# Two attentions on one core: how the second one's K is loaded, its scores are grouped and its Q is laid out

## The chip, the cores and the metric

The kernel runs on one core of a Trainium2 chip. The metric is the device time of one execution in microseconds (us); lower is better. The time before is 901.6 us, the median of three runs (900.64, 901.60 and 902.88).

## What is computed

Two attention blocks, A and B, work on separate inputs; their outputs stand side by side in the result. Both have 16 batches of 32 query tokens, model width 1024, 32 query heads of width 128, and a cache of 1024 keys. All tensors are bf16. A has 4 key/value heads, each shared by 8 query heads; B has 32.

```python
# B; A is the same, with k and v of each of 4 heads repeated for 8 query heads
q = (x @ wq).reshape(B, Sq, H, Dh).transpose(0, 2, 1, 3)
scores = einsum("bhqd,bhkd->bhqk", q, k_cache) * (Dh ** -0.5)
p = softmax(scores, axis=-1)
o = einsum("bhqk,bhkd->bhqd", p, v_cache)
b = o.transpose(0, 2, 1, 3).reshape(B, Sq, H * Dh) @ wo
return concatenate([a, b], axis=-1)
```

B's K and V are 134 MB each, A's 17 MB each; with the weights, the core's DMA engines read 337.64 MB from HBM (page).

## The kernel before

**The unit of work.** Scores of one "quad" fill 128 partitions (4 heads or head-batch pairs, of 32 query tokens each) by 1024 keys. Each attention has 128 quads. In A a quad is 4 query heads of one batch that share a key/value head; in B it is 2 batches times 2 heads, each with its own K and V. The steps of a quad are: scores on TensorE into one of two score buffers in PSUM (`ps_s`, two banks each, used in turn by all quads in the order in which they are recorded, `SBuf`), maximum on VectorE (`st_max`, L837), exponential with row sum on ScalarE (`st_exp`, L850), transposition of P on TensorE (L862), copy to SBUF (`st_pev`, through the helper at L526), P times V on TensorE (L884 for A, L892 for B), reciprocal (L901), scaling (L908 or L909), transposition of O (L914), copy (L526). After every 4 B quads or 8 A quads, `oproj` (L680) multiplies by a slice of `wo` and adds into an SBUF accumulator (L691, L694).

**B's scores before.** The head width has to be on partitions. `st_dmaK` loads, for one batch and two heads, 512 KB as 128 rows of 4096 B (16 keys per partition), two such loads to a quad. `KB_sb` holds 4 of them. VectorE transposes 32x32 blocks of 4-byte words (`st_ktrB`, L785; two instructions to a quad) into `KBt_sb`, which is double buffered by quad. After that the 128 elements of a head lie in two groups of 32 partitions and in two 2-byte halves, so that scores are sums of four matmuls on 32x32 tiles of the array: 32 matmuls of 512 columns to a quad (L827), recorded as 4 operations of 8. Their stationary rows, `QR`, need Q in the same broken-up order. `qprojB` (L616) computes Q with tokens on partitions (`Qtok`), `qprepB_tr` transposes it in 32x32 blocks on VectorE (`QBt`, L625; 32 times in all), and `qprepB_sh` moves it to the row groups by matmuls with the identity (L638, 512 matmuls of 256 columns), copied out to `QR` by ScalarE or VectorE (L526).

**V, A and weights.** V of a B quad comes in two loads of 512 KB with rows of 2048 B (L763), three quads deep. A's K and V are 256 KB loads with rows of 2048 B, two deep. `wq` comes in pieces with rows of 1024 B (L579), `wo` in rows of 2048 B.

**What sets the order.** The kernel records all operations with the buffers that they read and write. `list_schedule` then plays them through with a table of durations (`DUR`), of DMA costs by row size (`PACKET`), priorities (`PRIO_BONUS`) and a price for changing between matmul tile shapes (`PE_MODE`, `MODE_SWITCH`). The result is a fixed order on each engine; "any" operations get ScalarE or VectorE. Each engine executes its list in order and waits on semaphores where a buffer isn't ready. All loads are issued by SyncE (SP) in one list: a load whose buffer is not free holds up the loads behind it. A load is recorded when the last user of its buffer is: K behind the transposition, V behind the quad that has it last.

The main loop takes, per step, one B quad (`quadB_all`), about one A quad (`stepA`; A ends after 97% of the steps), a piece of Q preparation and projections, and weight loads.

Of the kernel before, what the change touches and what calls it, by code (L numbers as in the profile page):

```python
# [17 lines left out]
NKB_SLOTS = 2  # L18
# [7 lines left out]
PRIO_BONUS = {}  # L26
PE_MODE = {"scoresB": 2, "Qshuf": 2, "PVB": 1}
MODE_SWITCH = 0.05
# [8 lines left out]
    "OT_tr": (0.056, 0.22), "KTA_tr": (0.45, 0.22), "Qshuf": (0.107, 0.20), "qprojA": (0.432, 0.20), "qprojB": (0.432, 0.20),  # L37
    "oprojA": (0.432, 0.20), "oprojB": (0.432, 0.20), "xT_tr": (0.45, 0.22),
    "exp": (1.10, 0.12), "PT_ev@act": (0.466, 0.13), "norm@act": (0.25, 0.13), "OT_ev@act": (0.11, 0.13), "KTA_ev@act": (0.466, 0.13),
    "qA_ev@act": (0.47, 0.13), "qB_ev@act": (0.478, 0.13), "QR_ev@act": (0.252, 0.13), "acc0@act": (0.47, 0.13), "acc0@dve": (0.58, 0.12), "xT_ev@act": (0.90, 0.13),  # L40
    "o_fin@act": (0.47, 0.13),
    "KBt_tr": (1.126, 0.11), "max": (1.12, 0.11), "recip": (0.06, 0.11), "norm@dve": (0.23, 0.13), "PT_ev@dve": (0.58, 0.12),
    "OT_ev@dve": (0.08, 0.12), "KTA_ev@dve": (0.58, 0.12), "QBt_tr": (0.345, 0.10), "acc+": (0.58, 0.12), "accF": (0.59, 0.12),
    "qA_ev@dve": (0.58, 0.12), "qB_ev@dve": (0.58, 0.12), "xT_ev@dve": (0.60, 0.12), "o_fin@dve": (0.58, 0.12), "QR_ev@dve": (0.30, 0.12),
# [3 lines left out]
PACKET = {"kb_dma": (4096, 0.159), "wq_dma": (1024, 0.046)}  # L48
PACKET_DEFAULT = (2048, 0.084)
# [381 lines left out]
def build(nc, pa, pb, out):  # L431
# [34 lines left out]
    with stack:  # L466
# [7 lines left out]
        zeros = sb("zeros", [P, P], BF)  # L474
        id32 = sb("id32", [P, P], F32)
        z32 = sb("z32", [P, P], F32)
# [4 lines left out]
        Qtok = sb("Qtok", [P, 2, NG, CW], BF)  # L481
        QBt = sb("QBt", [P, CW], BF)
        QR = sb("QR", [P, 2, 4, 2, Dh], BF)
# [5 lines left out]
        KB_sb = sb("KB_sb", [P, 2 * NKB, 16 * Dh], BF)  # L489
        KBt_sb = sb("KBt_sb", [P, 2, 2, 16 * Dh], BF)  # L490
# [17 lines left out]
        if HOOK is not None:  # L508
            print("sbuf bytes remaining per partition:", nc.sbuf_bytes_remaining() if callable(nc.sbuf_bytes_remaining) else nc.sbuf_bytes_remaining)

        pr.add("pool", lambda g: g.memset(zeros[:], 0.0), writes=["zeros"], name="c0")
        pr.add("pool", lambda g: g.affine_select(ident[:], zeros[:], [[1, P]], ALU.not_equal, 1.0, base=0, channel_multiplier=-1),
               reads=["zeros"], writes=["ident"], name="c1")
        pr.add("pool", lambda g: g.memset(z32[:], 0.0), writes=["z32"], name="c0")
        pr.add("pool", lambda g: g.affine_select(id32[:], z32[:], [[1, P]], ALU.not_equal, 1.0, base=0, channel_multiplier=-1),
               reads=["z32"], writes=["id32"], name="c1")
# [90 lines left out]
        def qprojB(m_, G):  # L607
            lazy_flush(("wq", 1, m_))

            JS = 2 if DJ % 2 == 0 else 1  # L610
            v = Virt("bank", "pj")
            for j0 in range(0, DJ, JS):
                def e_qp(e, j0=j0):
                    last = None
                    for j in range(j0, j0 + JS):
                        last = e.matmul(bank(v)[:, 0:CW], xT_sb[:, 1, j, G * P:(G + 1) * P], wq_sb[:, 1, j, :], start=(j == 0), stop=(j == DJ - 1))  # L616
                    return last
                pcs = sorted(set(j * WQP // DJ for j in range(j0, j0 + JS)))
                pr.add("pe", e_qp, reads=[("wq", 1, k_) for k_ in pcs] + [("xT", 1, G)], writes=[v], claims=[("Qtok", m_ % 2, G)], name="qprojB", dur=0.225 * JS,
                       rtag=dict((("wq", 1, k_), m_) for k_ in pcs))  # L620
            evac(Qtok[:, m_ % 2, G, :], lambda: bank(v)[:, 0:CW], reads=[], writes=[v, ("Qtok", m_ % 2, G)], name="qB_ev",
                 wtag={("Qtok", m_ % 2, G): m_}, mul=scale)

        def qprepB_tr(m_, G):
            pr.add("dve", lambda e: e.transpose(QBt[:, :].bitcast(F32), Qtok[:, m_ % 2, G, :].bitcast(F32)),  # L625
                   reads=[("Qtok", m_ % 2, G)], writes=["QBt"], name="QBt_tr", rtag={("Qtok", m_ % 2, G): m_}, wtag={"QBt": (m_, G)})

        def qprepB_sh(m_, G, a_list):
            gp = (m_ * NG + G) % 2
            for a in a_list:  # L630
                v = Virt("bank", "pj")

                def e_sh(e, a=a, v=v):
                    last = None
                    for rg in range(4):
                        e_ = rg // 2
                        rhs = QBt[32 * a:32 * a + 32, :].rearrange("p (hp e x) -> p e hp x", hp=2, e=2)[:, e_, :, :]
                        last = e.matmul(bank(v)[32 * rg:32 * rg + 32, 0:2 * Dh].rearrange("p (hp x) -> p hp x", hp=2),  # L638
                                        ident[32 * a:32 * a + 32, 32 * a:32 * a + 32], rhs, start=True, stop=True,
                                        tile_position=(32 * a, 32 * rg))  # L640
                    return last
                pr.add("pe", e_sh, reads=["QBt", "ident"], writes=[v], claims=[("QR", gp, a)], name="Qshuf", rtag={"QBt": (m_, G)})
                evac(QR[:, gp, a, :, :], lambda v=v: bank(v)[:, 0:2 * Dh].rearrange("p (hp x) -> p hp x", hp=2), reads=[],
                     writes=[v, ("QR", gp, a)], name="QR_ev", wtag={("QR", gp, a): (m_, G)})

# [74 lines left out]
        def mk_quadB(t):  # L720
# [10 lines left out]
            q.kvslot = t % 2  # L731
            q.krslot = t % NKB
            q.vslot = t % NVB
            q.first_of_group = (jb == 0)
# [5 lines left out]
        def st_dmaK(q, t_=None):  # L740
# [6 lines left out]
            else:  # L747
                sl = (2 * q.t + t_) % (2 * NKB)
                ksrc = pb["k"][q.b0 + t_, q.h0:q.h0 + 2].rearrange("hh (p s) d -> (hh p) (s d)", s=16)
                pr.add("sp", lambda e: e.dma_start(KB_sb[:, sl, :], ksrc), writes=[("KB", sl)], dma_key=f"kb{sl}", name="kb_dma", dur=2 * Sk * Dh * 2, wtag={("KB", sl): q.kid})  # L750
# [31 lines left out]
        def st_ktrB(q, t_):  # L782
            sl = q.kvslot
            rs = (2 * q.t + t_) % (2 * NKB)
            pr.add("dve", lambda e: e.transpose(KBt_sb[:, sl, t_, :].bitcast(F32), KB_sb[:, rs, :].bitcast(F32)),  # L785
                   reads=[("KB", rs)], writes=[("KBt", sl, t_)], name="KBt_tr", rtag={("KB", rs): q.kid}, wtag={("KBt", sl, t_): q.kid})
# [8 lines left out]
        def st_scores(q):  # L795
# [3 lines left out]
            q.vbt, q.vbo = Virt("bank"), Virt("bank")  # L799
            vS = q.vS  # L800
            if q.pi == 0:
                sl = q.kvslot
                qt = QT_sb[:, q.s % 2]

                for u in range(2):
                    pr.add("pe", lambda e, u=u: e.matmul(ps_s[:, vS.idx, u, :], qt[:, q.b, q.hh0:q.hh0 + 4, :].rearrange("p a q -> p (a q)"),  # L806
                                                         KTA_sb[:, sl, u * 512:(u + 1) * 512], start=True, stop=True),
                           reads=[("QT", q.s % 2, q.hh0 + a) for a in range(4)] + [("KTA", sl)], writes=vS.res, name="scoresA", dur=0.225,
                           tag="A%d" % q.t, rtag=dict([(("QT", q.s % 2, q.hh0 + a), q.s) for a in range(4)] + [(("KTA", sl), q.kid)]))
            else:  # L810
                sl = q.kvslot
                gp = (q.m * NG + q.G) % 2

                def e_s(e, fp):
                    last = None
                    if True:
                        f, pd = fp // 2, fp % 2
                        o0 = f * 64 + pd
                        for t_ in range(2):
                            a = 2 * q.bp + t_  # L820
                            for hh in range(2):
                                cg = 2 * t_ + hh
                                for g2 in range(2):
                                    rg = 2 * hh + g2
                                    lhsT = QR[32 * rg:32 * rg + 32, gp, a, q.hp, o0:o0 + 63:2]
                                    rhs = KBt_sb[32 * rg:32 * rg + 32, sl, t_, :].rearrange("p (s x) -> p s x", s=16)[:, :, o0:o0 + 63:2]
                                    last = e.matmul(ps_s[32 * cg:32 * cg + 32, vS.idx, g2, :].rearrange("p (s j) -> p s j", s=16), lhsT, rhs,  # L827
                                                    start=(fp == 0), stop=(fp == 3), tile_position=(32 * rg, 32 * cg))
                    return last
                for fp_ in range(4):  # L830
# [105 lines left out]
        def nextA(t, k):  # L936
            later = [u for u in newA if u > t]
            return quadsA[later[k - 1]] if len(later) >= k else None

        def quadB_all(q):  # L940
            t = q.t
            for t_ in range(2):
                st_ktrB(q, t_)
                if t + NKB < NIT:
                    st_dmaK(quadsB[t + NKB], t_)
# [41 lines left out]
        for t_ in range(2):  # L987
            st_dmaK(quadsB[0], t_)
# [136 lines left out]
```

## Time and profile before

| quantity | value |
|---|---|
| median of three runs | 901.6 us |
| profiled execution: its span, first to last instruction | 902.6 us |
| instructions | 29455 |
| ScalarE / VectorE / TensorE busy | 610.8 / 745.3 / 836.3 us |
| loads and stores | 341.67 MB, mean 379 GB/s |
| K loads of B, issue to landing (median) | 9.2 us |
| V loads of B, issue to landing (median) | 8.1 us |
| mean granted TensorE clock | 0.985 |

The page of the profile gives the profiled execution by its span only; nothing that lies around it is recorded, so that the span stands for its time. It is 1.0 us over the median of the runs.

How to read it: a busy share is an average over the span. TensorE's matmuls are pipelined, so its busy time includes the depth of the pipeline. "DMA share" in a table of windows is the mean busy share of 16 DMA engines; it can pass 1 since packets overlap a little. A packet is one row of a load. The chain of waits goes back from the last instruction, step by step, to what released it.

### The profile page before, as it was taken

The numbers are of one execution on the slowest core, as the hardware profiler recorded it, in microseconds if no ns is written. First come the engines' busy times: TensorE is split into PE (matmuls) and PEld (weight loads), VectorE is DVE, ScalarE is ACT, GpSimd is POOL, SyncE is SP. The second block draws the span as 40 slices with busy tenths as digits, with TensorE's granted clock in tenths as the row PEclk, the third lists the DMA queues.
The fourth block names the chain that finished last, engine by engine and source line by source line (L and its number), as shares of the span: only waits on it lengthen the run. The fifth ranks groups of instructions, "written<-read, shape, count | busy, mean of one in ns | idle before, by whom it ended". The sixth has DMA issues, their size and how long they took to land.

```text
span 902.6 us, 29455 instructions
## 1 busy us (share of the span) xinstructions
PE 836.3 (93%) x12864; PEld 481.8 (53%) x12864; DVE 745.3 (83%) x1057; ACT 610.8 (68%) x1384; POOL 1.1 (0%) x8
## 2 busy tenths in 40 slices
PE   6999999999899999999999998999998988999886
PEld 4365555555555555555545455555555554555453
DVE  0578897888887999689887899878979788798885
ACT  3477886677666776676776466776867666586763
POOL 0000000000000000000000000000000000000000
PEclk9999999999999999999999999999999999999999
DMA  9999999999999999999999999999999999999994
GB/s 325 383 389 393 386 385 392 390 393 383 392 387 389 393 380 388 380 386 376 387 385 391 394 369 389 388 393 370 388 387 391 392 391 367 344 393 393 393 377 170
DMA packets 153984, 341.67 MB, mean 379 GB/s; under 512 B 12544, under 2 KB 28928, under 8 KB 153856
## 3 DMA queue, kind: packets, MB, share of 16 engines
q1 hardware_dynamic: 153856, 339.79, 100.6%
q8 instruction: 102, 1.67, 0.8%
q14 instruction: 26, 0.21, 0.1%
HBM read 337.64 MB, written 2.10 MB: 376 GB/s over the span
## 4 chain that ended last, share of the span: by engine, by line
PE 48%; DMA 23%; DVE 19%; ACT 8%; SPq 1%; issue 1%; ACTq 0%; DVEq 0%
DMA KB_sb<-in_B_k_cache_dram 21%; PE ps_s L827 10%; PE ps_g L862 9%; DVE stat L837 8%; DVE KBt_sb L785 8%; PE ps_g L680 6%; ACT P_sb L850 5%; PE ps_g L892 4%; PE ps_g L598 4%; PE ps_g L884 4%; PE ps_g L616 3%; PE ps_s L806 3%; PE ps_g L776 2%; ACT PT_sb L526 1%; PE ps_g L914 1%
## 5 line engine op out<-in xcount | busy, mean ns | idle before, releaser
L785 DVE STREAM_TRANSPOSE KBt_sb<-KB_sb 128x1024 f32<-128x1024 f32 x256 | 311.8, 1231 | 42.5 <-DMA KB_sb<-in_B_k_cache_dram 40.4
L837 DVE TENSOR_REDUCE stat<-ps_s 128x1 f32<-128x1024 f32 x256 | 304.7, 1209 | 50.7 <-PE ps_s L827 34.3
L850 ACT ACTIVATE P_sb<-ps_s,stat 128x1024 bf16<-128x1024 f32 x256 | 285.8, 1119 | 51.5 <-DVE stat L837 50.0
L862 PE MATMUL ps_g<-id,P_sb 128*128 128x128 f32 x1024 | 177.0, 300 | 13.0 <-ACT P_sb L850 4.7
L862 PEld LDWEIGHTS ps_g<-id,P_sb 128*128 128x128 f32 x1024 | 150.5, 207 | 54.9 <-issue 11.1
L827 PE MATMUL ps_s<-KBt_sb,QR 32*32 32x512 bf16 x4096 | 157.2, 399 | 19.5 <-ACT P_sb L850 10.9
L526 ACT COPY PT_sb<-ps_g 128x512 f32<-128x512 f32 x234 | 134.9, 591 | 59.5 <-PE ps_g L862 58.3
L908 ACT ACTIVATE O_sb<-ps_g,stat 128x128 bf16<-128x128 f32 x199 | 71.4, 370 | 63.0 <-PE ps_g L892 32.4
L806 PE MATMUL ps_s<-KTA_sb,QT_sb 128*128 128x512 bf16 x256 | 91.5, 388 | 6.0 <-ACT P_sb L850 5.6
L827 PEld LDWEIGHTS ps_s<-KBt_sb,QR 32*32 32x32 bf16 x4096 | 49.3, 90 | 81.1 <-ACT P_sb L850 17.8
L892 PE MATMUL ps_g<-VB_sb,PT_sb 128*32 128x128 bf16 x4096 | 91.1, 224 | 1.4 <-ACT PT_sb L526 0.9
L892 PEld LDWEIGHTS ps_g<-VB_sb,PT_sb 128*32 128x32 bf16 x4096 | 60.2, 97 | 48.7 <-issue 29.2
L884 PE MATMUL ps_g<-VA_sb,PT_sb 128*128 128x128 bf16 x1024 | 78.8, 220 | 1.8 <-ACT PT_sb L526 0.7
L884 PEld LDWEIGHTS ps_g<-VA_sb,PT_sb 128*128 128x128 bf16 x1024 | 61.6, 98 | 28.2 <-issue 8.5
L616 PE MATMUL ps_g<-wq_sb,xT_sb 128*128 128x512 bf16 x256 | 71.4, 386 | 2.9 <-DMA wq_sb<-in_B_wq_dram 2.8
L680 PE MATMUL ps_g<-woB_sb,OTB_sb 128*128 128x512 bf16 x256 | 68.7, 381 | 4.4 <-ACT OTB_sb L526 1.8
L598 PE MATMUL ps_g<-xT_sb,wq_sb 128*128 128x512 bf16 x256 | 72.0, 385 | 0.3
L680 PE MATMUL ps_g<-woA_sb,OTA_sb 128*128 128x512 bf16 x256 | 63.0, 380 | 1.3 <-DVE OTA_sb L526 1.0
L914 PE MATMUL ps_g<-ident,O_sb 128*128 128x128 bf16 x256 | 51.8, 224 | 3.0 <-ACT O_sb L908 2.0
L850 ACT ACTIVATION_READ_ACCUMULATOR P_sb<-ps_s,stat 128x1 f32 x256 | 51.8, 202 | 0.0
L526 ACT COPY OTA_sb<-ps_g 128x64 f32<-128x64 f32 x114 | 24.7, 216 | 36.7 <-PE ps_g L914 36.1
L691 DVE TENSOR_TENSOR acc<-acc,ps_g 128x512 f32<-128x512 f32 x64 | 41.2, 675 | 8.1 <-PE ps_g L680 7.6
(41 smaller groups left out, 537.5 us busy)
## 6 DMA issues: line engine op xcount, KB each, us to landing
VB_sb<-in_B_v_cache_dram SPq DMA_DIRECT2D x256, 512.0 KB, 8.1
KB_sb<-in_B_k_cache_dram SPq DMA_DIRECT2D x256, 512.0 KB, 9.2
KA_sb<-in_A_k_cache_dram SPq DMA_DIRECT2D x64, 256.0 KB, 7.7
VA_sb<-in_A_v_cache_dram SPq DMA_DIRECT2D x64, 256.0 KB, 8.1
wq_sb<-in_B_wq_dram SPq DMA_DIRECT2D x32, 256.0 KB, 8.6
wq_sb<-in_A_wq_dram SPq DMA_DIRECT2D x32, 256.0 KB, 8.8
woB_sb<-in_B_wo_dram SPq DMA_DIRECT2D x32, 256.0 KB, 9.2
woA_sb<-in_A_wo_dram SPq DMA_DIRECT2D x32, 256.0 KB, 9.1
```

The source lines that it names most:

```text
L526: return e.copy(dst, src) if hasattr(e, "activation") else e.tensor_copy(dst, src)
L598: last = e.matmul(bank(v)[:, 0:tn], wq_sb[:, 0, j, hc * Dh:(hc + 1) * Dh], xT_sb[:, 0, j, t0:t0 + tn], start=(j == 0), stop=(j == DJ - 1))
L616: last = e.matmul(bank(v)[:, 0:CW], xT_sb[:, 1, j, G * P:(G + 1) * P], wq_sb[:, 1, j, :], start=(j == 0), stop=(j == DJ - 1))
L680: last = e.matmul(bank(v)[:, 0:OUTW], OT[:, gp, hh, :], wo_[:, hh, oh * OUTW:(oh + 1) * OUTW], start=(hh == 0), stop=(hh == nh - 1))
L785: pr.add("dve", lambda e: e.transpose(KBt_sb[:, sl, t_, :].bitcast(F32), KB_sb[:, rs, :].bitcast(F32)), reads=[("KB", rs)], writes=[("KBt" ...
L806: pr.add("pe", lambda e, u=u: e.matmul(ps_s[:, vS.idx, u, :], qt[:, q.b, q.hh0:q.hh0 + 4, :].rearrange("p a q -> p (a q)"), KTA_sb[:, sl, ...
L827: last = e.matmul(ps_s[32 * cg:32 * cg + 32, vS.idx, g2, :].rearrange("p (s j) -> p s j", s=16), lhsT, rhs, start=(fp == 0), stop=(fp == 3 ...
L837: pr.add("dve", lambda e: e.tensor_reduce(stat[:, vst.idx, 0:1], ps_s[:, vS.idx, :, :], AXIS.XY, ALU.max, negate=True), writes=vS.res + [v ...
L850: return e.activation(dst, src, ACTF.Exp, bias=stat[:, vst.idx, 0:1], scale=1.0, accum_out=stat[:, vst.idx, 1:2])
L862: last = e.transpose(bank(vb)[:, m * P:(m + 1) * P], p32[:, m:Sk // 2:NPK], id32[:])
L884: last = e.matmul(bank(vb)[:, 0:Dh], ptc_of(vPT, c, 0, P), VA_sb[:, kvs, c, :], start=(c == 0), stop=(c == NCH - 1))
L892: last = e.matmul(bank(vb)[32 * a:32 * a + 32, 0:Dh], ptc_of(vPT, c, 32 * a, 32 * a + 32), VB_sb[:, kvs, a // 2, a % 2, c, :], start=(c == ...
```

## The change

K of B is loaded for one batch and four heads at once: 1 MB as 128 rows of 8192 B (32 keys per partition); `KB_sb` holds 3 of these. A pair of quads (the same two batches, heads 0-1 and 2-3 of the four) shares two loads. Their transposition is 4 instructions of the same size as before, each on one half (`u`) of the 32 keys; the read side now takes every second 4-byte word, so that after it a partition group belongs to one head. `KBt_sb` holds one pair, where it held two quads. The scores of both quads of a pair are recorded together, as 8 operations of 8 matmuls; they take both score buffers. `qprojB` makes Q with head elements on partitions straight away: `wq` is now the stationary side, taken at every fourth column, and the result is what the scores read (`QB_sb`). `Qtok`, `QBt`, `QR` and the steps that make them are gone. The order of P's columns for B changes with the keys' order (`st_exp`). Tables of the planner are changed.

```diff
-NKB_SLOTS = 2
+NKB_SLOTS = 3
-PRIO_BONUS = {}
-PE_MODE = {"scoresB": 2, "Qshuf": 2, "PVB": 1}
-MODE_SWITCH = 0.05
+PRIO_BONUS = {"max": 8, "exp": 8, "scoresA": 6, "scoresB": 6}
+PE_MODE = {"scoresB": 2, "PVB": 1}
+MODE_SWITCH = 0.1
...
-PACKET = {"kb_dma": (4096, 0.159), "wq_dma": (1024, 0.046)}
-PACKET_DEFAULT = (2048, 0.084)
+PACKET = {"kb_dma": (8192, 0.318), "wq_dma": (1024, 0.0487)}
+PACKET_DEFAULT = (2048, 0.0885)
...
-        KB_sb = sb("KB_sb", [P, 2 * NKB, 16 * Dh], BF)
-        KBt_sb = sb("KBt_sb", [P, 2, 2, 16 * Dh], BF)
+        KB_sb = sb("KB_sb", [P, NKB, 32 * Dh], BF)
+        KBt_sb = sb("KBt_sb", [P, 2, 32 * Dh], BF)
...
-        def qprojB(m_, G):
+        def qprojB(m_, fp):
...
-                        last = e.matmul(bank(v)[:, 0:CW], xT_sb[:, 1, j, G * P:(G + 1) * P], wq_sb[:, 1, j, :], start=(j == 0), stop=(j == DJ - 1))
+                        w = wq_sb[:, 1, j, fp:CW:4]
+                        last = e.matmul(bank(v)[:, 0:NTOK], w, xT_sb[:, 1, j, :], start=(j == 0), stop=(j == DJ - 1))
...
-            evac(Qtok[:, m_ % 2, G, :], lambda: bank(v)[:, 0:CW], reads=[], writes=[v, ("Qtok", m_ % 2, G)], name="qB_ev",
+            evac(QB_sb[:, m_ % 2, fp, :], lambda: bank(v)[:, 0:NTOK], reads=[], writes=[v, ("QB", m_ % 2, fp)], name="qB_ev",
...
-                sl = (2 * q.t + t_) % (2 * NKB)
-                ksrc = pb["k"][q.b0 + t_, q.h0:q.h0 + 2].rearrange("hh (p s) d -> (hh p) (s d)", s=16)
+                k = q.t + t_
+                sl = k % NKB
+                ksrc = pb["k"][q.b0 + t_, q.m * MS:(q.m + 1) * MS].rearrange("h (p s) d -> (h p) (s d)", s=32)
...
-            pr.add("dve", lambda e: e.transpose(KBt_sb[:, sl, t_, :].bitcast(F32), KB_sb[:, rs, :].bitcast(F32)),
+            c0, c1 = u * 16 * Dh, (u + 1) * 16 * Dh
+            pr.add("dve", lambda e: e.transpose(KBt_sb[:, t_, c0:c1].bitcast(F32).rearrange("p (s g i) -> p s g i", s=16, g=2),
+                                               KB_sb[:, sl, c0:c1].bitcast(F32).rearrange("p (s i g) -> p s g i", s=16, g=2)),
...
+        def st_scoresB(qs):
+            for q in qs:
+                st_slots(q)
+            def e_s(e, u, fp):
+                last = None
+                o0 = (fp // 2) * 64 + fp % 2
+                for t_ in range(2):
+                    for hh in range(2):
+                        cg = 2 * t_ + hh
+                        for q in qs:
+                            rg = 2 * q.hp + hh
+                            tok = (q.b0 + t_) * Sq
+                            lhsT = QB_sb[32 * rg:32 * rg + 32, q.m % 2, fp, tok:tok + Sq]
+                            rhs = KBt_sb[32 * rg:32 * rg + 32, t_, :].rearrange("p (s x) -> p s x", s=32)[:, 16 * u:16 * u + 16, o0:o0 + 63:2]
+                            last = e.matmul(ps_s[32 * cg:32 * cg + 32, q.vS.idx, u, :].rearrange("p (s j) -> p s j", s=16), lhsT, rhs,
+                                            start=(fp == 0), stop=(fp == 3), tile_position=(32 * rg, 32 * cg))
...
-                    dst = P_sb[:, vP.idx, :].rearrange("p (g j s) -> p g j s", g=2, s=16)
+                    dst = P_sb[:, vP.idx, :].rearrange("p (j u s) -> p u j s", u=2, s=16)
...
+        def pairB_front(n):
+            q0, q1 = quadsB[2 * n], quadsB[2 * n + 1]
+            for t_ in range(2):
+                for u in range(2):
+                    st_ktrB(q0, t_, u)
+                kdma(2 * n + t_ + NKB)
+            st_scoresB([q0, q1])
+            for q in (q0, q1):
+                st_max(q)
+                st_exp(q)
...
-            quadB_all(qB)
+            if t % 2 == 0:
+                pairB_front(t // 2)
+            quadB_back(qB)
```

## The prediction

> **What bounds the kernel now.** I read the page first: the busy rows, then the slices.
>
> ```profile
> PE 836.3 (93%) x12864; PEld 481.8 (53%) x12864; DVE 745.3 (83%) x1057; ACT 610.8 (68%) x1384; POOL 1.1 (0%) x8
> DMA  9999999999999999999999999999999999999994
> DMA packets 153984, 341.67 MB, mean 379 GB/s; under 512 B 12544, under 2 KB 28928, under 8 KB 153856
> q1 hardware_dynamic: 153856, 339.79, 100.6%
> ```
>
> Two resources look full, TensorE and the DMA engines. TensorE's figure counts pipeline depth; the DMA figure is plain: the packets of the load queue alone fill 16 engines for the whole span. The windows separate the ends from the middle:
>
> ```profile
> 0.00:15.00 15.00, 7.54 (x59) 4.41 (x60) 0.71 (x2) 6.02 (x7) 1.15 (x8) 0.99 0.88 293
> 30.00:870.00 840.00, 790.14 (x12323) 456.25 (x12323) 720.37 (x1025) 585.78 (x1336) 0.00 (x0) 0.99 1.03 386
> 622.00:626.00 4.00, 3.90 (x60) 1.84 (x59) 3.94 (x4) 1.34 (x4) 0.00 (x0) 1.00 0.72 251
> 885.00:902.60 17.60, 9.90 (x200) 5.73 (x188) 8.45 (x13) 6.45 (x16) 0.00 (x0) 0.89 0.29 103
> ```
>
> The last two columns are DMA share and GB/s. From 30 to 870 us the engines are full (1.03); single holes such as 622-626 us are rare; the end is a tail of compute. In the trace's packet records I counted, at each moment, by how much fewer than 16 packets were in flight: 2.5 us of idle before 15 us, 8.8 us from there to 885 us, 11.1 us after. That leaves 902.6 - 22.4 = 880.2 us in which the time is simply bytes over rate. The waits agree: VectorE stands 40.4 us before its K transposition for data, so compute is ahead of the loads.
>
> ```profile
> DVE KBt_sb L785 <- DMA KB_sb<-in_B_k_cache_dram: 40.4, 39, 8.6
> SPq L763 <- PE ps_g L892: 136.7, 69, 7.4
> SPq L750 <- DVE KBt_sb L785: 115.2, 77, 5.2
> ```
>
> The SP rows are loads held back until a buffer is free. With a median 9.2 us from issue to landing they mostly cost nothing; the 622-626 us hole is one that did: V waited 4.6 us at the head of SP's list and the engines ran dry.
>
> **The row size (on the path).** Stretches with almost only one kind of load give its rate:
>
> ```profile
> 33.00:35.50 2.50, 2.05 (x18) 0.86 (x15) 2.50 (x5) 1.80 (x4) 0.00 (x0) 1.00 1.09 349
> 20.20:22.70 2.50, 2.50 (x13) 1.17 (x12) 0.00 (x0) 0.00 (x0) 0.00 (x0) 1.00 1.05 386
> 24.90:27.40 2.50, 2.50 (x13) 1.08 (x12) 0.58 (x1) 0.12 (x1) 0.00 (x0) 1.00 1.03 410
> ```
>
> These are rows of 1024 B (wq), 2048 B (V) and 4096 B (K). A fit of packet counts to full stretches of 2 us over the whole trace gives 47, 85.4 and 162.8 ns a packet on one engine: 38.6 ns per KB and about 8 ns for the packet itself. On that line 8192 B cost 318 ns against 2 x 162.8 = 325.6: 7.7 ns less for each of 16,384 new packets, over 16 engines **-7.9 us**. The bounds are the only 8192 B packets in this trace, those of instruction loads on another queue: 307 ns before the stream starts (-19 us) and a median of 328 ns beside it (+2 us, no gain). I take the line, since it is the same queue and buffer; the 328 shares its engine with a second queue.
>
> The Trainium skill ("DMA: Bandwidth & Descriptors", section "Bandwidth", under small descriptors) gives a fixed 3 bus cycles per packet on top of one cycle per 32 B. By that a 4096 B row is 131 cycles and the saving 3 of 262, an estimate of 3.7 ns a packet, -3.8 us; the sum below would be 895. The three rates above ask for about twice that.
>
> **Q's preparation (beside it).** Gone are 32 transposes of 424 ns on VectorE (13.6 us), 512 identity matmuls (41.0 us of TensorE's busy time), and their copies: 101 on ScalarE, 381 ns each (37.8 us) and 27 on VectorE (11.0 us). The new projection has the same 256 matmuls of 512 columns. Its stationary columns are strided; the nearest row, P times V for A, has a stride of two and loads in 98 ns against 99 ns unstrided, and 256 loads even at the 207 ns of the 4-byte ones would add 28 us to an engine's load port that is 53% busy. All this lies under the loads: it moves the end by nothing. The planner spends part of it: by the orders of both kernels VectorE takes over 34 copies of P (682 ns each) and some smaller ones, 33 us, so VectorE goes from 745 to about 754 us and ScalarE falls by some 60.
>
> **The scores (beside it).** Still 4096 matmuls. Before they came in 179 groups among other work, now nearly always 64 in a row; changes of tile shape on TensorE fall from 790 to 389. A group of 32 takes 1.13 us of which the last 0.38 is depth. The trace shows the gap around a change as "issue" on the weight side, 0.42 us at a time, mostly under a running matmul; at some 0.15 to 0.2 us of real loss each, my estimate from those rows, TensorE gains 60 to 80 us of room. That should shorten what SP waits for.
>
> **The transposes.** Same count and size at 1231 ns, with a read stride of two words. No row of before strides VectorE's SBUF reads; I take no change, bounded by twice the time (below).
>
> **Holes in the load stream.** K's buffer grows from 2 to 3 MB, P times V is split less often (the 622 us hole was V behind a split one). But K is freed in lumps: two transposes free 1 MB, and the next pair's transposes wait for the burst, as `KBt_sb` is single. SP's list is in order, so V and A's loads stand behind such a K. I take half of the 8.8 us back, **-4** (bounds -8.8 and +8.8).
>
> **Ends.** The first loads are the same bytes: 0. At the end, the last transposes finished at 889.0 us and the rest of the quad took 13.6 us. Now a burst of 64 (about 1.9 us, not 1.13) and two maxima in a row (1.2 more) stand there: +2, less what half-bursts hide, **+1.5** (0 to +2.5).
>
> Sum: 902.6 - 7.9 - 4 + 1.5 = 892.2 in profile terms. The span is 1.0 over the median of the runs, so **891 us**.
>
> **Rivals.**
> 1. *Larger rows move no faster*, or are cut into 4096 B again (then the change doesn't do what it says). For it: the 328 ns. Against: the steady step from 349 to 386 to 410 GB/s. Time: 902.6 + 0 - 4 + 1.5 - 1 = 899.
> 2. *Lock-step, slower.* Both score buffers go to one burst and there is one `KBt_sb`, so during a burst VectorE has neither a maximum nor a free transpose to do. If nothing covers the burst, 1.9 us x 64 = 122 us of forced idle on top of 754 busy, plus 34 us that it idles at the two ends (25 in the first 30 us, 9 in the last 17.6): 910 us. It decides once the uncovered idle per pair passes (891 - 34 - 754) / 64 = 1.6 us. For it: VectorE is already 14.87 of 15 us busy in one window, and max, max, exponential (1.3), score, max, exponential follow each other. Against: that chain is 1.9 + 2.4 + 1.3 + 0.6 + 1.2 + 1.3, with gaps 9.2 us, of a 13.6 us period; 2 us of copies, sums and reciprocals per pair can fill the burst, and transposes of the next pair's first half can begin at mid-burst.
> 3. *Strided transposes.* At twice the time, 256 x 1024 words x 1.05 ns (the slope between 424 ns for 256 and 1231 for 1024) is 275 us: 754 + 275 + 34 = 1063. It decides above 0.4 us per instruction. The Trainium skill ("SBUF — State Buffer", Door 1, on cachelines) holds that two hits in a 16-byte line keep full bandwidth; a stride of two 4-byte words has two, so by it there is no price. No run here shows it yet.
>
> **How the numbers follow.** Forecast 0.62 (883 to 897), rival 1 0.18, rival 2 0.14, rival 3 0.06. A measurement of this kernel can tell about 0.3%, 2.7 us, from no change: faster is below 898.9, slower above 904.3. Rival 1 straddles the lower edge, so faster is 0.62 + 0.08, the same 0.10 + 0.03 of rival 2's near end, slower the rest, 0.17. The range leaves out rival 3 and most of rival 2: 882 to 906, the low end with packets near 310 ns or all holes gone.
>
> **What will show it.** Packets: 137,600 in all, 16,384 of them in the class from 8 KB up; 153,984 again would be rival 1's second form. Stretches with only K near 412 GB/s. The DMA row all 9s with a sum of idle near 5 us between the ends. L785's successor at 1.23 us; at 2.3 it is rival 3. If VectorE's idle time is before the maximum, released by the score burst, and more than 100 us in all, it is rival 2, and slices of DMA fall below 9. I am wrong if the load stream has holes of another origin, K behind its lumps at the head of SP's list.

## The result and the profile after

The changed kernel took **922.1 us** (median of four runs, 919.99 to 923.55) where the kernel before took 902.2 (four runs): a ratio of 1.0223 [1.0201 to 1.0245], **slower**. The forecast was 891 and the range ended at 906. The mechanism of rival 2, the lock-step, came; the 910 us put on it were 12 too few.

The page of the kernel after, the same rows as shown of before:

```profile
span 917.0 us, 28068 instructions
PE 784.1 (86%) x12234; PEld 485.4 (53%) x12352; DVE 746.8 (81%) x1055; ACT 563.7 (61%) x1226; POOL 1.1 (0%) x8
DMA  9999999999999999999999999999999999999993
DMA packets 135545, 341.57 MB, mean 372 GB/s; under 512 B 10496, under 2 KB 26880, under 8 KB 119040
q1 hardware_dynamic: 135424, 339.78, 98.5%
```

TensorE is busy for 52 us and ScalarE for 47 us *less* than before (118 of TensorE's 12,352 matmuls left no record, so its part is somewhat smaller), VectorE the same within 2 us, fewer packets move the same bytes, the slices of DMA are still all 9s, and the kernel is slower. Averages do not show why. The windows of the same kernel (length; then busy time of TensorE, its weight loads, VectorE, ScalarE and GpSimd; clock, DMA share, GB/s):

```profile
0.00:15.00 15.00, 3.39 (x29) 2.87 (x30) 1.85 (x2) 3.21 (x3) 1.14 (x8) 1.00 0.87 294
30.00:870.00 840.00, 733.02 (x11501) 452.48 (x11611) 707.53 (x1002) 529.26 (x1157) 0.00 (x0) 0.98 1.01 379
255.00:257.50 2.50, 1.35 (x6) 0.67 (x6) 2.36 (x4) 2.01 (x5) 0.00 (x0) 1.00 1.01 419
263.00:267.00 4.00, 3.95 (x74) 2.34 (x78) 4.00 (x5) 2.19 (x6) 0.00 (x0) 1.00 0.48 158
```

A stretch with only K (255 us) is *faster* than it was, 419 GB/s against 410. Such stretches scatter by some 10 GB/s; over all with more than 93% of their bytes from K, the median is 412 now and 406 before, so the larger rows bring a little. But the middle as a whole fell from 386 to 379 GB/s, by holes such as the one at 263 us. Counted from packet records as in the prediction (packets under 512 B left out, and up to the last packet of a load or store), idle of the load engines was, before 15 us / from there to 885 / after: 2.5 / 8.8 / 11.1 us before, 2.5 / 20.4 / 13.2 us now. The span without these is 880.2 before and 881.0 now. In both kernels it includes some 1.5 us between the last packet and the end.

The waits after (who waited, for whom, us in all, times, longest):

```profile
DVE KBt_sb L758 <- PE ps_s L802: 77.4, 60, 10.4
...
DVE KBt_sb L758 <- DMA KB_sb<-in_B_k_cache_dram: 6.9, 2, 6.0
```

Before, VectorE stood before its K transposition for *data*, 40.4 us. That wait is now 6.9 us, and one for the *score burst* stands in its place: 60 times (there are 64 pairs) and 77.4 us. The chain of waits by engine, first of the kernel before:

```profile
PE 48%; DMA 23%; DVE 19%; ACT 8%; SPq 1%; issue 1%; ACTq 0%; DVEq 0%
```

and the same row of after:

```profile
PE 43%; DVE 40%; ACT 11%; issue 4%; DMA 1%; SPq 1%; DVEq 0%; ACTq 0%
```

DMA has left the chain that sets the end, 23% to 1%, and VectorE has doubled its part.

The hole at 263 us shows the mechanism, which begins one pair earlier. From the same chain of after (start, duration, what; some steps left out):

```profile
244.36 1.17 PE ps_s L802 x22
...
245.63 4.63 DVE KBt_sb L758 x4
250.26 1.12 DVE stat L814
...
251.40 1.21 ACT P_sb L827 x2
...
257.98 1.11 ACT P_sb L827 x2
...
259.14 3.13 PE ps_s L802 x56
```

Read it down. A burst of 64 matmuls reads the only `KBt_sb`. VectorE's next instructions in its fixed list are the next pair's four transposes, which overwrite `KBt_sb`, so they start only when the burst's first half is done. Then the four run in a row, 4.6 us, while the two score buffers that the burst filled wait for their maxima until 250.2 us and for their exponentials until 251.4. A's scores need these buffers and come later too, and with them everything behind: P transposed, P times V, and the release of V's buffers. The loads that SyncE (SP) issues show it, and so does what the engines did in the next round (in brackets the idle time before and what ended it):

```profile
252.17 0.47 SPq L624 DMA_DIRECT2D woA_sb<-in_A_wo_dram  x1
258.95 0.34 SPq L729 DMA_DIRECT2D VA_sb<-in_A_v_cache_dram  x1
259.14 3.13 PE L802 MATMUL ps_s<-KBt_sb,QB_sb 32*32 32x512 bf16 x64 [0.22 <-ACT P_sb L827]
...
261.19 4.63 DVE L758 STREAM_TRANSPOSE KBt_sb<-KB_sb 128x1024 f32<-128x1024 f32 x4 [1.90 <-PE ps_s L802]
...
264.28 0.63 PE L869 MATMUL ps_g<-VB_sb,PT_sb 128*32 128x128 bf16 x32
...
264.96 1.10 SPq L735 DMA_DIRECT2D VB_sb<-in_B_v_cache_dram  x2
...
265.74 2.31 DVE L814 TENSOR_REDUCE stat<-ps_s 128x1 f32<-128x1024 f32 x2
```

SP issued nothing from 252.6 to 258.95 us, waiting for A's P times V to release a V buffer. Then B's V waited 4.2 us more, for a P times V (264.28) that stood behind the next burst on TensorE. In that time the loads ran dry (0.48 of full, above). The four transposes at 261.19, after 1.90 us of idle, hold up the next maxima in the same way. Not all of this hole is the lock's. This burst took 3.13 us, where the median of the 64 is 2.06, and from 259 to 261 us the granted clock was 0.50:

```profile
259.00:261.00 2.00, 1.86 (x40) 0.81 (x48) 0.16 (x1) 0.34 (x2) 0.00 (x0) 0.50 1.05 357
```

Only two other bursts took over 2.3 us. With two copies of `KBt_sb` the transposes would not have to wait for the burst.

### The profile page after: what moved, and what is told of

Its sections match the earlier page's. It is cut to its first block, busy times and chain, and to the rows that moved or that the text cites. A ratio compares the mean times of both kernels' runs of the same rounds, so it can differ in the third digit from the quotient of the medians.

```text
span 917.0 us, 28068 instructions
## 1 busy us (share of the span) xinstructions
PE 784.1 (86%) x12234; PEld 485.4 (53%) x12352; DVE 746.8 (81%) x1055; ACT 563.7 (61%) x1226; POOL 1.1 (0%) x8
## 2 busy tenths in 40 slices
DMA packets 135545, 341.57 MB, mean 372 GB/s; under 512 B 10496, under 2 KB 26880, under 8 KB 119040
## 4 chain that ended last, share of the span: by engine, by line
PE 43%; DVE 40%; ACT 11%; issue 4%; DMA 1%; SPq 1%; DVEq 0%; ACTq 0%
DVE KBt_sb L758 19%; DVE stat L814 16%; PE ps_s L802 10%; ACT P_sb L827 9%; PE ps_g L839 8%; PE ps_g L652 5%; PE ps_g L869 4%; PE ps_g L610 3%; PE ps_g L592 3%; PE ps_s L782 3%; PE ps_g L861 3%; PE ps_g L748 2%; DVE acc L663 2%; PE ps_g L891 1%; ACT PT_sb L520 1%
## 5 line engine op out<-in xcount | busy, mean ns | idle before, releaser
L758 DVE STREAM_TRANSPOSE KBt_sb<-KB_sb 128x1024 f32<-128x1024 f32 x256 | 301.5, 1219 | 84.3 <-PE ps_s L802 77.4
L814 DVE TENSOR_REDUCE stat<-ps_s 128x1 f32<-128x1024 f32 x256 | 300.0, 1203 | 23.9 <-PE ps_s L782 19.4
L520 ACT COPY PT_sb<-ps_g 128x512 f32<-128x512 f32 x200 | 115.5, 589 | 52.4 <-PE ps_g L839 51.0
L802 PE MATMUL ps_s<-KBt_sb,QB_sb 32*32 32x512 bf16 x4096 | 133.9, 390 | 8.1 <-ACT P_sb L827 6.2
L782 PE MATMUL ps_s<-KTA_sb,QT_sb 128*128 128x512 bf16 x236 | 75.4, 396 | 48.9 <-ACT P_sb L827 43.5
L802 PEld LDWEIGHTS ps_s<-KBt_sb,QB_sb 32*32 32x32 bf16 x4096 | 61.3, 90 | 60.8 <-ACT P_sb L827 10.2
L869 PE MATMUL ps_g<-VB_sb,PT_sb 128*32 128x128 bf16 x4096 | 85.3, 222 | 5.6 <-issue 4.2
L610 PE MATMUL ps_g<-xT_sb,wq_sb 128*128 128x512 bf16 x226 | 62.9, 380 | 5.6 <-DVE acc L663 2.7
L652 PE MATMUL ps_g<-woB_sb,OTB_sb 128*128 128x512 bf16 x236 | 63.8, 379 | 3.7 <-DVE OTB_sb L520 1.0
L592 PE MATMUL ps_g<-xT_sb,wq_sb 128*128 128x512 bf16 x226 | 62.7, 379 | 4.2 <-issue 1.9
L782 PEld LDWEIGHTS ps_s<-KTA_sb,QT_sb 128*128 128x128 bf16 x256 | 16.8, 99 | 78.6 <-ACT P_sb L827 75.0
```

Of the source, the lines that this page charges most:

```text
L520: return e.copy(dst, src) if hasattr(e, "activation") else e.tensor_copy(dst, src)
L592: last = e.matmul(bank(v)[:, 0:tn], wq_sb[:, 0, j, hc * Dh:(hc + 1) * Dh], xT_sb[:, 0, j, t0:t0 + tn], start=(j == 0), stop=(j == DJ - 1))
L610: last = e.matmul(bank(v)[:, 0:NTOK], w, xT_sb[:, 1, j, :], start=(j == 0), stop=(j == DJ - 1))
L652: last = e.matmul(bank(v)[:, 0:OUTW], OT[:, gp, hh, :], wo_[:, hh, oh * OUTW:(oh + 1) * OUTW], start=(hh == 0), stop=(hh == nh - 1))
L758: pr.add("dve", lambda e: e.transpose(KBt_sb[:, t_, c0:c1].bitcast(F32).rearrange("p (s g i) -> p s g i", s=16, g=2), KB_sb[:, sl, c0:c1]. ...
L802: last = e.matmul(ps_s[32 * cg:32 * cg + 32, q.vS.idx, u, :].rearrange("p (s j) -> p s j", s=16), lhsT, rhs, start=(fp == 0), stop=(fp == ...
```

## The experiments

Each kernel ran beside the kernel before on the same chip; ratios are to that. The theories at the start: (1) the single `KBt_sb` puts VectorE and TensorE in lock-step; (2) the harm is in one burst taking both score buffers, so that A's scores wait; (3) the planner's new tables made a worse order; (4) K in lumps of 1 MB holds up SP's list.

**A second `KBt_sb`.** The copy is chosen by `(q.t // 2) % 2`. The accumulators go to bf16 to make room in SBUF, which rounds the sums more.

```diff
-        KBt_sb = sb("KBt_sb", [P, 2, 32 * Dh], BF)
+        KBt_sb = sb("KBt_sb", [P, 2, 2, 32 * Dh], BF)
-        acc = sb("acc", [P, 2, NG, D], F32)
+        acc = sb("acc", [P, 2, NG, D], BF)
```

> The changed kernel with KBt_sb double buffered by pair; the output accumulators are kept in bf16 instead of f32 to make room (the sums are rounded more often; nothing else changes). Theory 1, the single KBt_sb is the lock: VectorE's 77 us of waiting for the score burst before a transpose falls below 20 us, the holes in the load stream go from 20 us back to under 9, and the time is 893 to 906. Theory 2, the hold of one burst on both score buffers is the lock: VectorE's wait only moves to the maxima, and the time stays at 915 to 923. Theory 3, the planner's new tables make a worse order: no change beyond 5 us, 917 to 925. Theory 4, K in lumps of 1 MB holds up SP's list: 917 to 925.

906.6 us, 1.0043 [1.0018 to 1.0067]. VectorE's longest waits in this kernel:

```profile
DVE stat L816 <- PE ps_s L803: 49.0, 27, 8.6
DVE KBt_sb L759 <- DMA KB_sb<-in_B_k_cache_dram: 23.6, 31, 6.2
```

and its chain by engine:

```profile
PE 42%; DVE 28%; DMA 16%; ACT 8%; issue 4%; SPq 2%; ACTq 0%; DVEq 0%
```

The transposes wait for the burst not once; they wait for data again, and DMA is back in the chain. Idle in the loads is 7.9 us from 15 to 870 us, and the span without idle 872.6. Part of VectorE's wait moved to the maxima, 49.0 us where it was 3.9, as theory 2 has it, but the time fell, which theories 2, 3 and 4 excluded. Theory 1 had said 906 at most. It is not yet faster than before: 21.9 us of idle stand after 870 us (before: 11.6). That the bf16 sums have no part in it took a control, the same edit of `acc` without the second `KBt_sb`, in the order of the kernel after:

> The changed kernel with only the output accumulators in bf16, in the same order on every engine: the control for the run with the double KBt_sb. If that run's gain came from KBt_sb (theory 1): 917 to 925, as the changed kernel, with the 677 ns additions into the accumulators no shorter. If it came from the bf16 accumulators: 904 to 909.

921.9 us, 1.0205 [1.0187 to 1.0222], as after; the transposes again wait 78.4 us for the burst, 60 times. So the 15 us are the second buffer's, together with the order that the planner makes for it: the order was not held fixed.

**Scores by quad.** `KBt_sb` stays single; the burst is cut into one for each quad.

```diff
-            st_scoresB([q0, q1])
             for q in (q0, q1):
+                st_scoresB([q])
                 st_max(q)
```

> The changed kernel with the scores recorded for one quad at a time, 8 operations of 4 matmuls, so that a quad takes only its own score buffer; single KBt_sb as in the change. Theory 2 (both buffers held): the wait of A's scores for the exponential falls by half from 75 us and the time is 900 to 912. Theory 1 (single KBt_sb): KBt_sb is held longer, until the second quad's scores, so the time is 920 to 945. A quad now uses two of four row groups; if these serialise, its 32 matmuls take up to twice 1.1 us and the time goes up by some 10 us for that alone.

967.6 us, 1.0709 [1.068 to 1.0737]: slower by far more than either theory allowed. From the waits of this kernel:

```profile
DVE KBt_sb L758 <- PE ps_s L802: 44.2, 54, 10.6
```

and from its page the busy row:

```profile
PE 885.7 (92%) x12199; PEld 507.3 (52%) x12352; DVE 784.1 (81%) x1091; ACT 542.7 (56%) x1190; POOL 1.1 (0%) x8
```

What A waits for (its scores on the exponential) fell from 75.0 to 27.3 us, as theory 2 wants, and the time rose by 45. Theory 2 gets no support here, nor is it refuted, since the kernel mixes two effects: a quad alone uses two of the four row groups (TensorE's busy time is up by 102 us, B's score matmuls alone from 133.9 to 251.8), and `KBt_sb` is held until the second quad. They were not separated.

**The planner's tables.** The kernel after with the old tables, and the kernel before with the new ones:

```diff
-PRIO_BONUS = {"max": 8, "exp": 8, "scoresA": 6, "scoresB": 6}
-MODE_SWITCH = 0.1
+PRIO_BONUS = {}
+MODE_SWITCH = 0.05
...
-PACKET_DEFAULT = (2048, 0.0885)
+PACKET_DEFAULT = (2048, 0.084)
```

> The changed kernel planned with the priorities, the price of a tile change and the packet costs of V and weights of before. Theory 3 (tables): at most 907. Theories 1, 2 and 4: within 6 us of the changed kernel, 916 to 928, with VectorE's wait for the burst still above 60 us.

> The kernel before, planned with the new priorities, price of a tile change and packet costs of V and weights. Theory 3 (tables): 912 or more. The others: 899 to 906.

1019.6 us, 1.1277 [1.1239 to 1.1315], and 939.9 us, 1.0402 [1.0365 to 1.0438]. No theory came near the first; the second is what theory 3 expected. The same tables save the changed kernel 97 us and cost the kernel before 36. From the waits of the kernel after with old tables:

```profile
ACT PT_sb L520 <- PE ps_g L839: 237.3, 142, 4.7
DVE KBt_sb L758 <- PE ps_s L802: 90.2, 63, 10.3
```

The wait for the burst is only 13 us longer; ScalarE now waits 237 us for transposed P (51 before). So theory 3 is wrong in sign for the changed kernel: with the new tables it is faster, not slower. The four runs with old tables also had a lower granted clock, 0.931 to 0.936 against 0.980 to 0.985 of after; how much of the 97 us goes with that was not tried. Two more kernels ask which entries matter: after with only the old packet costs of V and the weights, and before with only the new priorities.

> The changed kernel planned with the packet costs of before for V and weights (0.084 and 0.046 us, where the change has 0.0885 and 0.0487); priorities and price of a tile change stay new. Theory 1 (single KBt_sb): the lock is in the buffers, so 912 to 928 whatever loads the planner counts on. Theory 3 in the form that the new packet costs pace the order to loads that are slower than the real ones: 900 to 908.

> The kernel before with the new priorities alone. All three new table entries together took it to 940. If the priorities did that, by drawing maxima, exponentials and scores ahead of the transposes and of P times V, which free K's and V's buffers: 930 to 950. If the price of a tile change or the packet costs did it: 899 to 910.

915.6 us, 1.0124 [1.008 to 1.0168], with 73.5 us of waiting for the burst: the packet costs are not what saves 97 us. And 954.3 us, 1.0573 [1.0533 to 1.0614]: the priorities alone cost the kernel before more than all tables together. VectorE's longest wait in that kernel:

```profile
DVE KBt_sb L785 <- PE ps_s L827: 77.3, 85, 3.2
```

and SP's:

```profile
SPq L750 <- DVE KBt_sb L785: 222.9, 140, 6.7
```

The first row does not exist in the kernel before (with all new tables it is 61.0 us), and the second was 115.2 us: K's buffers come free later. The priorities did not push the transposes back, though. Between the start of a quad's transposes and the end of the scores that used the same buffer before, the median is 0.1 us, and 6.0 in the kernel before; between the end of the transposes and their own scores it is 9.8 us, and 0.7 before. So the transposes stand far ahead of their use in VectorE's list and wait there for their buffer. The wait on the score burst can be made by order alone, even with two buffers.

**Are the priorities needed with two buffers?** The kernel with two `KBt_sb` and an empty `PRIO_BONUS`:

> Double KBt_sb (accumulators in bf16) planned with no priorities; the rest of the tables as in the change. With a single KBt_sb the old tables cost 100 us. If the priorities are there to keep the lock-step short (theory 1), they hardly matter once KBt_sb is double: 898 to 912. If paired bursts need them in any case: 940 or more.

897.7 us, 0.9942 [0.9918 to 0.9967]: 5 us *faster* than before. Without the wait for the burst the priorities are a cost of 9 us (1.0043 against 0.9942).

**A version that beats both.** Two `KBt_sb`, priorities kept, packet costs between the old and the new, and `LOOK` lower (the time by which the planner may pass over the operation that can start first, for one with more work behind it).

```diff
-LOOK = 0.35
+LOOK = 0.15
-PACKET = {"kb_dma": (8192, 0.318), "wq_dma": (1024, 0.0487)}
-PACKET_DEFAULT = (2048, 0.0885)
+PACKET = {"kb_dma": (8192, 0.318), "wq_dma": (1024, 0.0475)}
+PACKET_DEFAULT = (2048, 0.0868)
```

> Double KBt_sb (accumulators in bf16), planned with packet costs 0.0868 and 0.0475 us, between those of before and after, and a look-ahead of 0.15 us for 0.35. If the loads are the only bound once the lock is gone, the opened end of the run with the double KBt_sb (21.9 us of idle DMA engines after 870 us, 11.6 in the kernel before) can be had back: 892 to 898, under the kernel before. If the end is longer by the nature of pairs, 902 to 908.

**892.8 us**, 0.9884 [0.9865 to 0.9902]. The window of its middle:

```profile
30.00:870.00 840.00, 744.54 (x11845) 474.51 (x11961) 720.21 (x1016) 546.79 (x1207) 0.00 (x0) 0.98 1.03 391
```

and VectorE's longest wait:

```profile
DVE KBt_sb L759 <- DMA KB_sb<-in_B_k_cache_dram: 38.6, 29, 6.6
```

391 GB/s where before had 386 and after 379, and VectorE waits for data, as it did in the kernel before. Is it the planner's numbers or the buffer? The same numbers with one `KBt_sb`, and the kernel before with the same `LOOK` and costs of V and the weights:

> The single KBt_sb planned as the fast kernel was: look-ahead 0.15 us, packet costs 0.0868 and 0.0475. If the double KBt_sb is what the fast kernel needs: 905 to 925, with VectorE's wait for the burst above 50 us. If the planner's numbers were all of it: 890 to 897.

> The kernel before planned with that look-ahead and those packet costs for V and weights. If the fast kernel's gain is its own (rows, fewer tile changes, no Q preparation): 899 to 912. If a better plan would do as much for the kernel before: 888 to 897.

930.5 us, 1.0283 [1.0245 to 1.0322], and 915.6 us, 1.0128 [1.0102 to 1.0155]. The numbers help neither alone; both kernels came out slower than was expected for either case. From the waits with one buffer:

```profile
DVE KBt_sb L758 <- PE ps_s L802: 83.7, 61, 9.6
```

At equal tables the second `KBt_sb` is worth 1.0283 less 0.9884, 4.0% or 36 us.

**The row size by itself.** The fastest version in the same order, but each row of K lands as two of 4096 B with a gap of 32 B:

```diff
-        KB_sb = sb("KB_sb", [P, NKB, 32 * Dh], BF)
+        KB_sb = sb("KB_sb", [P, NKB, 2, 16 * Dh + 16], BF)
```

> The same kernel in the same order, but each row of 8192 B lands as two of 4096 B with 32 bytes between them in SBUF, so that the packets are 4096 B again. Row theory: a packet costs 320 ns at 8192 B and 2 x 162.8 at 4096 B, 5.6 ns a packet less, so this run is 5 to 8 us slower than its twin. Rival, that larger rows bring nothing: within 2 us of it.

897.8 us, 0.993 [0.9912 to 0.9948], 5.0 us over its twin. The page of this kernel:

```profile
DMA packets 151929, 341.57 MB, mean 383 GB/s; under 512 B 10496, under 2 KB 26880, under 8 KB 151808
```

The packets are there again: 151,929 less 135,545 is 16,384. The fit of packet times gives 160.3 ns for 4096 B in this kernel and 317.0 for 8192 B in its twin, a saving of 3.6 ns for each new packet, or 3.7 us over 16 engines. Such a fit moves by a nanosecond with the stretches that are taken as full: with another choice it is 159.1 and 313.6, a saving of 4.6 ns. The span without idle differs by 2.5 us (873.6 and 871.1).

| kernel | `KBt_sb` | median us | ratio to before | wait of K's transposes for the burst, us |
|---|---|---|---|---|
| before | 2 quads | 902.2 | 1 | none |
| after | 1 pair | 922.1 | 1.0223 | 77.4 |
| after, sums in bf16 | 1 pair | 921.9 | 1.0205 | 78.4 |
| after, old V and weight packet costs | 1 pair | 915.6 | 1.0124 | 73.5 |
| after, old tables | 1 pair | 1019.6 | 1.1277 | 90.2 |
| after, scores by quad | 1 pair | 967.6 | 1.0709 | 44.2 |
| after, `LOOK` 0.15 and middle packet costs | 1 pair | 930.5 | 1.0283 | 83.7 |
| after with two `KBt_sb` | 2 pairs | 906.6 | 1.0043 | none |
| after with two `KBt_sb`, no priorities | 2 pairs | 897.7 | 0.9942 | none |
| after with two `KBt_sb`, `LOOK` 0.15 and middle packet costs | 2 pairs | 892.8 | 0.9884 | none |
| the same, K landing in rows of 4096 B | 2 pairs | 897.8 | 0.993 | none |

Every kernel of the changed layout with the wait in the last column is at 915 us or more, and each without it at 907 or less.

## Why the prediction was wrong

**The step that failed** is the one that set the lock-step aside: "that chain is 1.9 + 2.4 + 1.3 + 0.6 + 1.2 + 1.3, with gaps 9.2 us, of a 13.6 us period". It follows one pair from burst to burst as if VectorE went straight from the burst to the maxima. Its list does not. In the order after, 33 times for 64 pairs four or more transposes stand between one maximum and the next, and they cannot start before the burst has let go of `KBt_sb`. Those 4.6 us (245.63 and 261.19 us above) belong to the chain: 9.2 + 4.6 = 13.8 us, and nothing is left of 13.6. The bursts of after did follow each other every 13.8 us (the first starts at 26.0 us, the last one's last matmul at 899.6, some 2 us into the burst: 63 intervals). That the two agree to a tenth is luck, since only half of the pairs have that order; that the slack was gone is not. Four transposes in a row are no harm by themselves: with two `KBt_sb` they stand between two maxima 40 times, in the fastest kernel 49 times, and never wait for a burst. With the old tables they do so once, and the transposes wait 90.2 us all the same. It is the wait for the burst at their head that ties them into the chain.

The reply "transposes of the next pair's first half can begin at mid-burst" was right, and worth little: at 261.19 us they do begin at mid-burst, after 1.90 us of idle, and then hold up the maxima. The prediction's sign for rival 2 was therefore set on the wrong instruction: before the maxima VectorE waited only 3.9 us for the burst, before the transposes 77.4, and the slices of DMA stayed at 9.

**Rival 2 had the mechanism and a wrong condition.** It was to decide when VectorE's uncovered idle passes 1.6 us a pair, and to cost 122 us of idle. This wait measured 77.4 / 64 = 1.2 us a pair, below the point, and it decided anyway; VectorE's idle time of every kind was 917.0 - 746.8 = 170.2 us. The condition asked whether VectorE *alone* gets full. It was busy 746.8 us of 917. What is full is a loop through VectorE, TensorE and ScalarE (40, 43 and 11% of the chain), where each waits for the next; no busy row shows it. So 910 was too low, from a sum of wrong parts: 122 + 754 + 34, where the runs have 77.4 for the wait, 746.8 for the work, and waits of other kinds that the sum leaves out.

**Holes: forecast -4, measured +11.6** (8.8 to 20.4 us), outside the bounds of ±8.8 that were set for it. The bad case named there, K in lumps at the head of SP's list (theory 4), is not it. SP's waits after:

```profile
SPq L735 <- PE ps_g L869: 254.3, 86, 10.3
...
SPq L721 <- DVE KBt_sb L758: 40.7, 23, 6.3
```

K's own wait fell from 115.2 to 40.7 us; V waits, 254.3 us after 136.7. But this sum alone proves nothing: it is 228.7 us in the fastest kernel. What a wait at the head of SP's list costs is the packets in flight when it ends, and that only the count of idle shows (6.5 us there from 15 to 870 us).

**Rows: forecast -7.9, measured -2.5 to -5.0.** The direction was right and the line through the three rates was too steep: 3.6 or 4.6 ns a packet by the fits, 4.9 by the 5.0 us between the medians, not 7.7. The prediction cited the Trainium skill ("DMA: Bandwidth & Descriptors", section "Bandwidth"): 3 bus cycles per packet, estimated there at 3.7 ns and -3.8 us. The twin kernels are nearer to that estimate than to the line, with a little more than it says. In the kernel after itself the saving does not show: its span without idle is 0.8 us longer than before. Why is open.

**End: forecast +1.5, measured +2.1** (idle after 885 us from 11.1 to 13.2), within its bounds of 0 to 2.5.

**Sum.** Of the profiled executions, 0.8 + 11.6 + 2.1 is +14.4 up to rounding, which is 917.0 - 902.6. Both had a granted clock of 0.985. The medians differ by 19.9; the profiled execution of after was the shortest of its four runs, 919.99 us, and each run of after took 1.75 to 3.0 us more than its own span. So the span does not stand for the time, as the text ahead of the prediction had it, and the forecast should have added some 2 us to its span, not taken 1.0 off.

**Priced at nothing, rightly:** the strided transposes (rival 3) and the removed Q preparation. L758 of after, beside 1231 ns for L785:

```profile
L758 DVE STREAM_TRANSPOSE KBt_sb<-KB_sb 128x1024 f32<-128x1024 f32 x256 | 301.5, 1219 | 84.3 <-PE ps_s L802 77.4
```

Taking some 50 us from TensorE and 47 from ScalarE did not keep the kernel from getting slower while the loop was the bound. With two `KBt_sb` the changed kernel gains more than the rows (892.8 against 902.2, -9.4, where rows are worth 5.0 at most), which points to some of that room being used there; it was not tried by itself. The Trainium skill ("SBUF — State Buffer", Door 1, on cachelines), by which this stride has no price, agrees with the 1219 ns.

**Priced at nothing, wrongly:** the tables. The effect of their entries here runs from -97 to +51 us, and it had another sign with one `KBt_sb` than with two.

**Open:** whether the priorities or `MODE_SWITCH` save the 97 us, and what the lower clock has in them; what the second buffer brings in an order that is held fixed; which part of the 102 us of TensorE's busy time in the split scores is row groups and which is waiting inside the pipeline; and why two `KBt_sb` at the new tables leave 21.9 us of idle after 870 us, which the other tables bring down to 12.3 in the fastest.

## What to carry to other kernels

When two units of work are merged, list the buffers that the merged unit holds until its end, and follow VectorE's (or any engine's) list in its fixed order behind the one that waits: what stands *between* the wait and the next step of the chain is part of the chain. A buffer that one engine fills and another reads in one long burst is the first candidate for a second copy, which was worth 15 to 36 us here. A second copy is no guarantee, since an order can bring the wait back, as the priorities did in the kernel before. And a planner's tables belong to one structure: compare two structures each with its own, since a set that saves one of them 97 us cost the other 36.

## What the runs showed of the hardware

- 8192 B rows of K streamed at 419 GB/s in a stretch of their own, 4096 B rows at 410 (medians of such stretches 412 and 406); by fits one packet on one engine took 47, 85.4, 159 to 163 and 314 to 320 ns for 1, 2, 4 and 8 KB.
- A 32x32 transposition of 4-byte words with a read stride of two words took 1219 ns, contiguous 1231. The stationary `wq` columns at a step of four loaded in 114 ns, against 99.
- Besides K's 16,384, another 2,048 packets went, all of 4 B. The kernel before issues 784 loads and stores and after 656; 16 times these are 12,544 and 10,496, the page's counts under 512 B. So there is one small packet for each load or store and engine. The kernel with rows of 4096 B has as many loads as after, and 10,496 again.
- In two kernels the time of the runs goes with the granted clock, in others only roughly: after took 919.99, 921.25, 923.00 and 923.55 us at 0.985, 0.983, 0.982 and 0.980; with the old packet costs it took 910.04, 912.85, 918.37 and 921.46 us at 0.983, 0.979, 0.970 and 0.967. Which of the two follows from the other, no run shows.
